# A Fourier mix and a maxout layer on one core: batch 0's first stage in two halves of output rows, and GpSimd's start-up work in another order

## The chip, the cores and the metric

The kernel runs on 1 core of one Trainium2 chip. The metric is the time of one execution on the device in microseconds; the time before is the median of 3 runs, 405.07 us (405.0 to 405.21). A profile is of one execution. Times inside it are counted from its first instruction.

Short names: PE is TensorE (matmuls; PEld its weight loads), DVE is VectorE, ACT is ScalarE, POOL is GpSimd, SP is SyncE, which here only asks for DMAs.

## The reference

```python
X = np.fft.fft(x, axis=1)          # x: 8 batches, 3072 positions, 256 channels, float32
X = np.fft.fft(X, axis=2)
t = X.real.astype(np.float32).reshape(24576, 256)
h = np.maximum(np.maximum(t @ w1, t @ w2), t @ w3)    # 256 -> 768
out = (h @ w_out).astype(np.float32)                   # 768 -> 256
```

## The kernel before, in words

**The work of one batch.** The Fourier transform over 3072 positions is split into 24 by 128. Stage one (`Mix.s`, seven pieces k = 0 to 6) multiplies x, as the stationary operand of 96 rows (4 channel groups of 24 positions) by 128 columns, with small constant matrices of at most 96 columns; the result is evicted into `z`. Stage two (`Mix.k`, pieces 0 to 5) multiplies `z` with the sine and cosine table `tabs` and gives `t`, the halves tE and tO. The transform over the channels is folded into the weights: `prep_first` multiplies the differences d2 = w2 - w1 and d3 = w3 - w1 (held in `d2_bf`, `d3_bf`; `differences`, line 231, makes them) with the matrix `md` and leaves `gE`, `gO` and `gD`, one of each for d2 and for d3. It does so for the halves jh = 0 and jh = 1 of the 768 columns, the second inside the unit loop. `prep_second` makes the folded output weights `gw` from `w1` and `w_out`.

**The unit loop.** For each of 8 batches there are 3 blocks of 512 tokens, and for each of them 6 units (jc). A unit (`unit_plus`) is four matmuls into two PSUM tiles, `pse2` and `pse3`; `unit_out` takes them out: ACT writes the Relu of `pse2` into `stmp` (line 605), then DVE takes the maximum of `stmp` and `pse3` (line 606). One unit later, two `gD` matmuls (`unit_minus`) turn the same PSUM tiles into the mirrored tokens, and `unit_out` runs again. `l2_block` multiplies with `w_out` and stores the rows, half of them through an indirect DMA that POOL issues with the row numbers in `rows_m`.

**What sets the order.** The schedule is manual on all five engines: each engine runs its instructions in the order in which the program emits them, and waits on semaphores. `plan` says behind which unit a side piece (stage one and two of the next batch, transposing copies, table pieces) is emitted. For batch 0, unit 2 emits `tab_sines(10, 13, (0,))` on ACT, which reads the table angles `w_late` that POOL's `tab_angles(10, 13)` has written; unit 4 emits the matmuls that read `wout_bf`.

**The start, which the diff touches.** Batch 0's x comes through POOL's DMA queue in three parts of positions bb (rows 0 to 40, 40 to 80, 80 to 112; four DMAs each, one per channel group), and the last 16 rows through SP and ACT. Each part is laid out twice by ACT and DVE, forward into `xn0` (`lay_rows`) and reversed into `xr0` (`turn_rows`). Behind x, POOL asks for w1; SP asks for the four pieces of w2 and w3 (`raw_w`: w2 and w3 of jh = 0, then of jh = 1) once the ninth of x's twelve DMAs (`last_part[0]`) has landed. 28 matmuls on dummy data (line 774) run until x is laid out. Then PE runs stage one, and behind its pieces stand d2 and d3 of jh = 0 on DVE, d2 and d3 of jh = 1 on POOL, the DMA for `w_out` and `tab_angles(10, 13)` on POOL. POOL's order before them is: a marker that waits for x's layout (line 460), four memsets, `store_rows` (the row numbers for the stores, lines 278 to 288), `tab_minus(7, 10)` (line 343).

**A pool that closes.** `pidx`, `rows_f` and `late`, which `store_rows` reads and writes, are tiles of the pool `gen`. That pool is closed before the unit loop, and the pools opened behind it (`h_pool` with `stmp`, `hp` and `hm` among them) take its place in SBUF:

```python
gen_pool_cm.__exit__(None, None, None)      # line 802
ps_s_cm.__exit__(None, None, None)
...
h_pool = ctx.enter_context(tc.tile_pool(name="hbuf", bufs=2))
```

Of the kernel before, what the change touches and what calls it, by code (L numbers as in the profile page):

```python
# [9 lines left out]
FP32 = mybir.dt.float32  # L10
# [3 lines left out]
ALU = mybir.AluOpType  # L14
# [19 lines left out]
def kernel(  # L34
# [221 lines left out]
    iota(pidx, [[0, 1]], cm=1)  # L256
    j128 = gen.tile([128, 128], FP32, tag="j128")
    iota(j128, [[1, 128]])
    for (r0, r1) in ((0, 40), (40, 80), (80, 112)):
        last_part = load_rows(nc.gpsimd, x0v[:, r0:r1, :], 0, r0, r1)  # L260

    def load_w(eng, wdst, wsrc, jh):
        return eng.dma_start(
            out=cols(wdst, jh),
            in_=wsrc.rearrange("(fc p) j -> p fc j", fc=2)[:, :, jh * 384:(jh + 1) * 384])

    for jh in range(2):
        load_w(nc.gpsimd, w1_bf, moe_w1, jh)
    for jh in range(2):
        for wsrc, wdst in zip((moe_w2, moe_w3), raw_w):  # L270
            ld = load_w(nc.sync, wdst, wsrc, jh)
            if jh == 0:
                tc.add_manual_dep(ld.ins, last_part[0].ins.name, AFTER, reason="x first")

    rows_f = gen.tile([128, 7 * B], FP32, tag="rows_f")
    late = gen.tile([128, 1], FP32, tag="late")
# [135 lines left out]
    def turn_rows(copy, r0, n, d0, d1):  # L412
        return reverse(copy, xr0, x0_first[:, r0 * 64:(r0 + n) * 64], r0, n, d0, d1)
# [32 lines left out]
    turn_rows(on_dve, 39, 40, 32, 65)  # L446
    lay_rows(on_act, bf_rows(40, 40), 40, 40, 12, 33)
    second_laid = lay_rows(on_dve, bf_rows(40, 40), 40, 40, 0, 12)
    for (copy, a, b, c, d) in ((on_act, 55, 64, 21, 33), (on_dve, 32, 55, 0, 21)):
        third_turned = turn_rows(copy, 79, 33, a, b)  # L450
        if copy is on_act:
            turn_rows(copy, 79, 32, 64, 65)
        laid = lay_rows(copy, bf_rows(80, 32), 80, 32, c, d)
    nc.vector.tensor_scalar(out=sgn, in0=pidx, scalar1=0.0, scalar2=None, op0=ALU.is_equal)
    nc.vector.tensor_scalar(out=sgn, in0=sgn, scalar1=2.0, scalar2=-1.0,
                            op0=ALU.mult, op1=ALU.add)
    nc.vector.tensor_scalar(out=dif, in0=sgn, scalar1=1.0, scalar2=None, op0=ALU.subtract)
    for ch in range(4):
        raw[1, ch] = load_chunk(1, ch)
    first_op = nc.gpsimd.memset(mark, 0.0)  # L460
    tc.add_manual_dep(first_op.ins, laid.ins.name, AFTER, reason="the two share a port")
    nc.gpsimd.memset(two_row, 0.0)
    nc.gpsimd.memset(two_row[0:1], 2.0)
    nc.gpsimd.memset(gw[:, 512:513], 0.0)
    nc.gpsimd.memset(gw[0:1, 512:513], 1.0)
    store_rows()
    tab_minus(7, 10, nc.gpsimd)

    def wide(t, cs):
        return t.rearrange("p (fc j) -> p fc j", fc=2)[:, :, cs]  # L470

    def prep_first(jh, bank):

        cs = slice(jh * 384, (jh + 1) * 384)
        for i, wv in enumerate((d2_bf, d3_bf)):
            for half in range(2):
                psg = bank()
                hs = slice(half * 128, (half + 1) * 128)
                for fc in range(2):
                    nc.tensor.matmul(  # L480
                        psg[:, 0:384], md[fc][:, hs],
                        wv[:, fc * DFF + jh * 384: fc * DFF + jh * 384 + 384],
                        start=(fc == 0), stop=(fc == 1))
                if half == 0:
                    nc.vector.tensor_copy(out=gE[i][:, cs], in_=psg[:, 0:384])
                else:
                    nc.scalar.copy(out=gO[i][:, cs], in_=psg[:, 0:384])
                    nc.vector.tensor_scalar(out=gD[i][:, cs], in0=psg[:, 0:384], scalar1=dif,
                                            scalar2=None, op0=ALU.mult)
                yield  # L490

    def prep_second():
# [30 lines left out]
    class Mix:  # L523
# [4 lines left out]
            self.tE = self.t[:, 0, :]  # L528
            self.tO = self.t[:, 1, :]

        def s(self, k, x0, pool=ps_f, evict=nc.scalar.copy):

            ps1 = pool.tile([128, 512], FP32, name="ps1", tag="ps")
            if k < len(DLS):
                parts = [(d, 96, m24f, m24r) for d in range(*DLS[k])]
            else:
                parts = [(0, 52, m0f, m0r), (32, 48, m24f, m24r), (1, 96, m24f, m24r)]
            c0 = 0
            for (d, n, mf, mr) in parts:
                if isinstance(x0, tuple):  # L540
                    pairs = ((x0[0](d), mf), (x0[1](d), mr))
                elif d:
                    pairs = ((x0[:, d, :], mf),)
                else:
                    pairs = ((x0[:, 0, :], mf), (x0[:, 33, :], mr))
                for i, (st, mv) in enumerate(pairs):
                    nc.tensor.matmul(ps1[:, c0:c0 + n], st, mv[:, 0:n], start=(i == 0),  # L547
                                     stop=(i == len(pairs) - 1))
                c0 += n
            if k < len(DLS):  # L550
                lo = 4 * DLS[k][0]
                evict(out=z[:, lo:lo + 20, 0:24],  # L552
                      in_=ps1[:, 0:480].rearrange("p (c r) -> p c r", r=24))
            else:
                evict(out=z_all[:, 0:52], in_=ps1[:, 0:52])
                evict(out=z[:, 2:8, 0:24],
                      in_=ps1[:, 52:196].rearrange("p (c r) -> p c r", r=24))

        def k(self, q, evict=nc.scalar.copy, pool=ps_f):

# [24 lines left out]
    def unit_plus(te, to, jc, n):  # L585
# [4 lines left out]
        for (pse, i) in ((pse2, 0), (pse3, 1)):  # L590
            nc.tensor.matmul(pse[:, 0:n], gE[i][:, js], te, start=True, stop=False)  # L591
            nc.tensor.matmul(pse[:, 0:n], gO[i][:, js], to, start=False, stop=True)  # L592
        return pse2, pse3
# [175 lines left out]
                l2_queue.pop(0)  # L769

    warm = ps_s.tile([128, 512], FP32, name="warm", tag="ps")
    for (n, after) in ((23, None), (3, second_laid), (2, third_turned)):
        for i in range(n):
            mm = nc.tensor.matmul(warm, tab[:, 0:128], tab[:, 0:512], start=True, stop=True)
            if after is not None and i == 0:
                tc.add_manual_dep(mm.ins, after.ins.name, AFTER, reason="warm until x is laid out")
    m = Mix(0)
    x0f = (lambda d: xn0[:, d, 0:128], rows_back(xr0))
    for k in range(7):
        m.s(k, x0f, pool=ps_s if k % 4 else ps_f,  # L780
            evict=nc.vector.tensor_copy if k in (1, 3) else nc.scalar.copy)
        if k == 1:
            halves = [t.rearrange("p (q two g) -> p two q g", two=2, g=4) for t in md]
            nc.vector.tensor_copy(out=halves[1][:, 0], in_=halves[0][:, 0])
            nc.vector.tensor_scalar(out=halves[1][:, 1], in0=halves[0][:, 1], scalar1=-1.0,
                                    scalar2=None, op0=ALU.mult)
            differences(nc.vector, 0, (0,))
        if k == 3:
            first_half = differences(nc.vector, 0, (1,))
            differences(nc.gpsimd, 1, after=first_half)  # L790
            nc.gpsimd.dma_start(out=wout_bf.rearrange("p (jc c) -> p jc c", jc=NJC),
                                in_=moe_w_out.rearrange("(jc p) c -> p jc c", jc=NJC))
# [100 lines left out]
    for b in range(B):  # L893
# [15 lines left out]
        for blk in range(3):  # L909
# [5 lines left out]
                for t, fl in zip((tE, tO), flipped):  # L915
                    nc.gpsimd.tensor_copy(fl, t[:, 3 * TOKB - 1: 2 * TOKB - 1: -1])
            for jc in range(NJC):
                pses = unit_plus(tE[:, cs], tO[:, cs], jc, TOKB)
# [52 lines left out]
```

## Time and profile before

| | |
|---|---|
| median of 3 runs | 405.07 us |
| the profiled execution | 404.64 us |
| its span, first to last instruction | 402.9 us |
| PE busy in the span | 386.0 us (96%) |
| DVE, ACT, POOL busy | 308.9, 265.5, 292.0 us |
| first dummy matmul | 10.01 us |
| first matmul of stage one | 18.67 us |
| first matmul of the unit loop | 24.18 us |

The profiled execution's time is 1.7 us over its span: what lies around the first and the last instruction. It is 0.43 us under the median. Rows of the timeline read: start, duration, engine, line, operation, output tile <- input tiles, shapes, count; in square brackets the engine's idle time before it and what ended it. A row with a count merges neighbours that are the same.

### The profile page before, as it was taken

The page shows a single profiled execution, that of the slowest core. Times are in us where ns is not written, and L with a number is a line of the kernel's source. Part 1 is how long each engine was busy: PE and PEld are TensorE (multiplying, and loading weights), DVE is VectorE, ACT ScalarE, POOL GpSimd, SP SyncE. Part 2 cuts the span into 40 slices and gives each one's busy share as a digit, 9 for nine tenths or more (in the row PEclk, how much of TensorE's full clock was granted, in tenths as well). Part 3 has the DMA queues.
Part 4 walks back from the last instruction along what each step waited for, and adds up shares of the span by engine and source line. Part 5 has one row for each costly group of instructions (what it writes and reads, how often), then busy time and mean ns, then how long its engine had stood idle before and what let it go on. Part 6 is the DMA issues. An engine that isn't in the chain of part 4 may idle for free.

```text
span 402.9 us, 8560 instructions
## 1 busy us (share of the span) xinstructions
PE 386.0 (96%) x2829; PEld 260.6 (65%) x2877; DVE 308.9 (77%) x556; ACT 265.5 (66%) x489; POOL 292.0 (72%) x394
## 2 busy tenths in 40 slices
PE   0999999999999999999999999999999999999996
PEld 0465667666676667666666666666677676666665
DVE  8898776788777877687776887787777877678884
ACT  6787767655866667756766677666766676655550
POOL 9599889879986998679877888768967524323521
PEclk9999999999999999999999999999999999999999
DMA  9989897789778838875478928886234411211214
GB/s 117 188 199 179 157 226 197 174 213 196 186 197 214 192 120 217 193 184 159 114 200 186 227 78 222 197 191 179 81 103 114 123 55 74 84 52 54 103 57 156
DMA packets 127597, 62.06 MB, mean 154 GB/s; under 512 B 111616, under 2 KB 116736, under 8 KB 126976
## 3 DMA queue, kind: packets, MB, share of 16 engines
q1 hardware_dynamic: 101976, 42.21, 42.3%
q0 software_dynamic: 24640, 18.98, 23.8%
q8 instruction: 22, 0.36, 0.4%
q10 hardware_dynamic: 936, 0.33, 0.3%
q14 instruction: 23, 0.19, 0.2%
HBM read 33.74 MB, written 29.88 MB: 158 GB/s over the span
## 4 chain that ended last, share of the span: by engine, by line
PE 85%; DVE 4%; DMA 3%; POOL 2%; ACT 2%; issue 2%; DVEq 0%; SPq 0%; POOLq 0%; ACTq 0%
PE po L616 29%; PE pse L591 16%; PE pse L599 14%; PE pse L592 12%; PE ps L571 3%; PE ps L573 3%; PE po L640 3%; PE pl L629 2%; PE ps L547 2%; POOL x L111 2%; DMA raw_w<-in_moe_w_dram 2%; DVE hm L606 2%; ACT stmp L605 2%; DMA x<-in_x_dram 2%; DVE other L643 1%
## 5 line engine op out<-in xcount | busy, mean ns | idle before, releaser
L605 ACT ACTIVATE stmp<-pse 128x512 bf16<-128x512 f32 x288 | 170.8, 600 | 52.6 <-PE pse L592 26.2
L606 DVE TENSOR_TENSOR hp<-pse,stmp 128x512 bf16<-128x512 f32 x144 | 99.5, 691 | 80.1 <-ACT stmp L605 51.8
L646 POOL TENSOR_TENSOR even<-even,other 128x256 f32<-128x256 f32 x92 | 70.1, 762 | 74.5 <-DVE other L643 74.2
L591 PE MATMUL pse<-t,gE 128*128 128x512 bf16 x288 | 109.1, 379 | 2.5
L606 DVE TENSOR_TENSOR hm<-pse,stmp 128x512 bf16<-128x512 f32 x144 | 99.2, 689 | 3.3 <-ACT stmp L605 3.1
L592 PE MATMUL pse<-t,gO 128*128 128x512 bf16 x249 | 94.3, 379 | 0.0
L616 PE MATMUL po<-wout_bf,hp 128*128 128x256 bf16 x576 | 85.9, 272 | 0.0
L616 PE MATMUL po<-wout_bf,hm 128*128 128x256 bf16 x570 | 85.3, 273 | 0.3
L599 PE MATMUL pse<-t,gD 128*128 128x512 bf16 x279 | 83.7, 379 | 0.1
L677 POOL DMA_INDIRECT out_dram<-ot,rows_m x53 | 53.8, 1015 | 20.2 <-DVE ot L670 10.7
L616 PEld LDWEIGHTS <-hp 128*128 128x128 bf16 x576 | 56.3, 98 | 17.3 <-issue 2.5
L616 PEld LDWEIGHTS <-hm 128*128 128x128 bf16 x576 | 56.4, 98 | 16.5
L670 DVE TENSOR_TENSOR ot<-po,even 128x512 f32<-128x512 f32 x92 | 62.8, 682 | 0.0
L173 POOL CAST xw<-xs 96x544 bf16<-96x544 f32 (+1 forms) x48 | 53.2, 1120 | 0.0
L178 POOL CAST xb<-xs 96x512 bf16<-96x512 f32 x48 | 52.4, 1100 | 0.0
L575 ACT CAST t<-ps 128x512 bf16<-128x512 f32 x48 | 27.9, 585 | 34.8 <-PE ps L573 34.7
L599 PEld LDWEIGHTS <-gD 128*128 128x128 bf16 x288 | 28.1, 98 | 32.2
L643 DVE SCALAR_TENSOR_TENSOR other<-twice,po 128x256 f32<-128x256 f32 x92 | 43.8, 476 | 0.1
L592 PEld LDWEIGHTS <-gO 128*128 128x128 bf16 x288 | 28.1, 98 | 20.4 <-issue 1.9
L591 PEld LDWEIGHTS <-gE 128*128 128x128 bf16 x288 | 28.2, 98 | 19.5 <-issue 0.7
L552 ACT CAST z_all<-ps 128x480 bf16<-128x480 f32 x46 | 24.8, 560 | 22.0 <-PE ps L547 21.9
L632 ACT COPY even<-pl 128x512 f32<-128x512 f32 x46 | 27.0, 587 | 9.7 <-PE pl L629 8.6
(178 smaller groups left out, 370.9 us busy)
## 6 DMA issues: line engine op xcount, KB each, us to landing
xs<-in_x_dram SPq DMA_DIRECT2D x84, 198.0 KB
out_dram<-ot SPq DMA_DIRECT2D x39, 256.0 KB
xs<-in_x_dram SPq DMA_DIRECT2D x28, 192.0 KB
held<-xb SPq DMA_DIRECT2D x48, 96.0 KB
xw<-held POOLq DMA_DIRECT2D x24, 192.0 KB
raw_w<-in_moe_w_dram SPq DMA_DIRECT2D x4, 384.0 KB
out_dram<-ot SPq DMA_DIRECT2D x12, 128.0 KB
x<-in_x_dram POOLq DMA_DIRECT2D x8, 120.0 KB
```

The lines of the kernel that those rows point to most:

```text
L173: nc.gpsimd.tensor_copy(v[:, d0:d1, ch * 32:ch * 32 + 32], xs[:, 0:32 * 64].rearrange("p (bb dl) -> p dl bb", dl=64)[:, d0:d1, :])
L178: nc.gpsimd.tensor_copy(mir[:, d0:d1, c0:c0 + 32], bass.AP(xs.tensor, xs.offset + 33 * 64 - 1 - d0, [xs.ap[0], [-1, d1 - d0], [-64, 32]]))
L591: nc.tensor.matmul(pse[:, 0:n], gE[i][:, js], te, start=True, stop=False)
L592: nc.tensor.matmul(pse[:, 0:n], gO[i][:, js], to, start=False, stop=True)
L599: nc.tensor.matmul(pse, gD[i][:, js], to, start=False, stop=True, skip_group_check=True)
L605: nc.scalar.activation(out=stmp[:, 0:n], in_=pses[0][:, 0:n], func=AX.Relu)
L606: nc.vector.tensor_tensor(out=dst, in0=src3, in1=stmp[:, 0:n], op=ALU.max)
L616: nc.tensor.matmul(po, hcols(jc), wout_bf[:, jc * 256:(jc + 1) * 256], start=False, stop=(jc == NJC - 1), skip_group_check=True)
L643: nc.vector.scalar_tensor_tensor(out=other, in0=twice, scalar=po[:, 256:257], in1=po[:, 0:256], op0=ALU.mult, op1=ALU.subtract)
L646: nc.gpsimd.tensor_tensor(out=line[:, 256:512], in0=line[:, 0:256], in1=other, op=ALU.add)
L670: nc.vector.tensor_tensor(out=parts, in0=po.rearrange("p (i c) -> p i c", i=2), in1=lin.rearrange("p (i c) -> p i c", i=2), op=ALU.add)
L677: stored(nc.gpsimd.indirect_dma_start(out.rearrange("(n two) c -> n (two c)", two=2) if pair else out, bass.IndirectOffsetOnAxis(ap=rows_m ...
```

## The change

Batch 0's stage one is made in two passes over its seven pieces, with seven PSUM banks open (`banks_s`). `s_half` with `sooner` makes 64 columns of x forward (rows 0 to 64) into PSUM partitions 0 to 63 and 64 columns reversed into partitions 64 to 127; these need x's rows up to 64 only. One dummy matmul waits for the third part's reversal. `s_half` with `later` adds the other 64 columns of each, crosswise, and after each piece `s_out` evicts it, odd pieces by DVE and even ones by ACT. Instead of 66 matmuls with 128 stationary columns there are 132 with 64.

x's parts are cut at row 84 instead of 80. SP asks for the weight pieces, w3's ahead of w2's, once the eighth x DMA (`parts_first[3]` of the second part) has landed.

d3 of jh = 0 moves from DVE to POOL, ahead of everything else there but the marker; d2 of jh = 0 stays on DVE, behind the evictions of stage one; on POOL follow d3 and d2 of jh = 1. The four memsets and `sgn` and `dif` go ahead of the marker on POOL. `store_rows` and `tab_minus(7, 10)` go behind the differences. `prep_first` takes d3 ahead of d2, and for jh = 0 makes both `gD` products at its end. Unit 0 takes `pse3` ahead of `pse2`. Stage two's piece 1 is evicted by DVE.

```diff
-    for (r0, r1) in ((0, 40), (40, 80), (80, 112)):
-        last_part = load_rows(nc.gpsimd, x0v[:, r0:r1, :], 0, r0, r1)
+    for (r0, r1) in ((0, 40), (40, 84), (84, 112)):
+        parts_first = load_rows(nc.gpsimd, x0v[:, r0:r1, :], 0, r0, r1)
+        if r0 == 40:
+            before_last = parts_first[3]
...
+    nc.gpsimd.tensor_scalar(out=sgn, in0=pidx, scalar1=0.0, scalar2=None, op0=ALU.is_equal)
+    nc.gpsimd.tensor_scalar(out=sgn, in0=sgn, scalar1=2.0, scalar2=-1.0,
+                            op0=ALU.mult, op1=ALU.add)
+    nc.gpsimd.tensor_scalar(out=dif, in0=sgn, scalar1=1.0, scalar2=None, op0=ALU.subtract)
+    nc.gpsimd.memset(two_row, 0.0)
+    nc.gpsimd.memset(two_row[0:1], 2.0)
+    nc.gpsimd.memset(gw[:, 512:513], 0.0)
+    nc.gpsimd.memset(gw[0:1, 512:513], 1.0)
     for jh in range(2):
-        for wsrc, wdst in zip((moe_w2, moe_w3), raw_w):
+        for wsrc, wdst in ((moe_w3, raw_w[1]), (moe_w2, raw_w[0])):
             ld = load_w(nc.sync, wdst, wsrc, jh)
             if jh == 0:
-                tc.add_manual_dep(ld.ins, last_part[0].ins.name, AFTER, reason="x first")
+                tc.add_manual_dep(ld.ins, before_last.ins.name, AFTER, reason="x first")
...
-            turn_rows(copy, 79, 32, 64, 65)
-        laid = lay_rows(copy, bf_rows(80, 32), 80, 32, c, d)
+            turn_rows(copy, 83, 28, 64, 65)
+        laid = lay_rows(copy, bf_rows(84, 28), 84, 28, c, d)
+
+    def sooner(d):
+        return xn0[:, d, 0:64], (xr0[:, 32 - d, 64:128] if d else xr0[:, 32, 65:129])
+
+    def later(d):
+        return xn0[:, d, 64:128], (xr0[:, 32 - d, 0:64] if d else xr0[:, 32, 1:65])
...
     tc.add_manual_dep(first_op.ins, laid.ins.name, AFTER, reason="the two share a port")
-    nc.gpsimd.memset(two_row, 0.0)
-    nc.gpsimd.memset(two_row[0:1], 2.0)
-    nc.gpsimd.memset(gw[:, 512:513], 0.0)
-    nc.gpsimd.memset(gw[0:1, 512:513], 1.0)
-    store_rows()
-    tab_minus(7, 10, nc.gpsimd)
...
-        for i, wv in enumerate((d2_bf, d3_bf)):
+        for i, wv in ((1, d3_bf), (0, d2_bf)):
...
-                    nc.vector.tensor_scalar(out=gD[i][:, cs], in0=psg[:, 0:384], scalar1=dif,
-                                            scalar2=None, op0=ALU.mult)
+                    scaled.append((gD[i][:, cs], psg[:, 0:384]))
+                if half and (jh or not i):
+                    for (dst, product) in scaled:
+                        nc.vector.tensor_scalar(out=dst, in0=product, scalar1=dif,
+                                                scalar2=None, op0=ALU.mult)
+                    scaled = []
...
+        def s_half(self, k, rows, ps1):
+
+            begin = rows is sooner
+            if k < len(DLS):
+                parts = [(d, 96, m24f, m24r) for d in range(*DLS[k])]
+            else:
+                parts = [(0, 52, m0f, m0r), (32, 48, m24f, m24r), (1, 96, m24f, m24r)]
+            c0 = 0
+            for i, (d, n, mf, mr) in enumerate(parts):
+                for j, (st, mv) in enumerate(zip(rows(d), (mf, mr))):
+                    p0 = 64 * j if begin else 64 - 64 * j
+                    nc.tensor.matmul(ps1[p0:p0 + 64, c0:c0 + n], st, mv[:, 0:n],
+                                     start=begin and i == 0,
+                                     stop=not begin and i == len(parts) - 1,
+                                     skip_group_check=True)
+                c0 += n
...
-    for (n, after) in ((23, None), (3, second_laid), (2, third_turned)):
...
+    warm_up(22)
     m = Mix(0)
...
+    for k in range(7):
+        m.s_half(k, sooner, banks_s[k])
+    warm_up(1, third_turned)
+    for k in range(7):
+        m.s_half(k, later, banks_s[k])
+        m.s_out(k, banks_s[k], nc.vector.tensor_copy if k % 2 else nc.scalar.copy)
         if k == 1:
...
-            differences(nc.vector, 0, (0,))
-        if k == 3:
-            first_half = differences(nc.vector, 0, (1,))
-            differences(nc.gpsimd, 1, after=first_half)
-            nc.gpsimd.dma_start(out=wout_bf.rearrange("p (jc c) -> p jc c", jc=NJC),
-                                in_=moe_w_out.rearrange("(jc p) c -> p jc c", jc=NJC))
-            tab_angles(10, 13, nc.gpsimd)
+            differences(nc.gpsimd, 0, (1,))
+    first_half = differences(nc.vector, 0, (0,))
+    differences(nc.gpsimd, 1, (1, 0), after=first_half)
+    store_rows()
+    tab_minus(7, 10, nc.gpsimd)
+    nc.gpsimd.dma_start(out=wout_bf.rearrange("p (jc c) -> p jc c", jc=NJC),
+                        in_=moe_w_out.rearrange("(jc p) c -> p jc c", jc=NJC))
+    tab_angles(10, 13, nc.gpsimd)
...
-    m.k(1, pool=ps_s)
+    m.k(1, pool=ps_s, evict=nc.vector.tensor_copy)
```

More of the change, by code (lines that the diff above doesn't have):

```diff
@@ L445 @@
     nc.scalar.activation(out=md[0], in_=vm, func=AX.Sin, scale=float(-2.0 * math.pi / 256.0))
-    turn_rows(on_dve, 39, 40, 32, 65)
-    lay_rows(on_act, bf_rows(40, 40), 40, 40, 12, 33)
-    second_laid = lay_rows(on_dve, bf_rows(40, 40), 40, 40, 0, 12)
+    turn_rows(on_dve, 39, 44, 32, 65)
+    lay_rows(on_act, bf_rows(40, 44), 40, 44, 12, 33)
+    lay_rows(on_dve, bf_rows(40, 44), 40, 44, 0, 12)
+    halves = [t.rearrange("p (q two g) -> p two q g", two=2, g=4) for t in md]
+    nc.vector.tensor_copy(out=halves[1][:, 0], in_=halves[0][:, 0])
+    nc.vector.tensor_scalar(out=halves[1][:, 1], in0=halves[0][:, 1], scalar1=-1.0,
+                            scalar2=None, op0=ALU.mult)
     for (copy, a, b, c, d) in ((on_act, 55, 64, 21, 33), (on_dve, 32, 55, 0, 21)):
-        third_turned = turn_rows(copy, 79, 33, a, b)
+        third_turned = turn_rows(copy, 83, 29, a, b)
         if copy is on_act:
-            turn_rows(copy, 79, 32, 64, 65)
-        laid = lay_rows(copy, bf_rows(80, 32), 80, 32, c, d)
[L454 to L457, printed above, removed]
+            turn_rows(copy, 83, 28, 64, 65)
[4 more added lines that the diff above has]
+        return xn0[:, d, 64:128], (xr0[:, 32 - d, 0:64] if d else xr0[:, 32, 1:65])
     for ch in range(4):
@@ L487, in prep_first @@
                     nc.scalar.copy(out=gO[i][:, cs], in_=psg[:, 0:384])
-                    nc.vector.tensor_scalar(out=gD[i][:, cs], in0=psg[:, 0:384], scalar1=dif,
-                                            scalar2=None, op0=ALU.mult)
+                    scaled.append((gD[i][:, cs], psg[:, 0:384]))
+                if half and (jh or not i):
+                    for (dst, product) in scaled:
+                        nc.vector.tensor_scalar(out=dst, in0=product, scalar1=dif,
+                                                scalar2=None, op0=ALU.mult)
+                    scaled = []
                 yield
@@ L529, in __init__, with s @@
             self.tO = self.t[:, 1, :]
-        def s(self, k, x0, pool=ps_f, evict=nc.scalar.copy):
+        def s(self, k, x0, pool=ps_f):
             ps1 = pool.tile([128, 512], FP32, name="ps1", tag="ps")
@@ L549, in s, with s_out @@
                 c0 += n
+            self.s_out(k, ps1)
+        def s_out(self, k, ps1, evict=nc.scalar.copy):
             if k < len(DLS):
@@ L583, in end, with unit_plus @@
             nc.scalar.copy(out=t_mid[:, :, self.b], in_=ps3[:, 0:2])
-    def unit_plus(te, to, jc, n):
+    def unit_plus(te, to, jc, n, swap=False):
         js = slice(jc * 128, (jc + 1) * 128)
@@ L589, in unit_plus @@
         pse3 = ps_l1.tile([128, TOKB], FP32, name="pse3", tag="pse3")
-        for (pse, i) in ((pse2, 0), (pse3, 1)):
+        for (pse, i) in ((pse2, 0), (pse3, 1)) if swap is False else ((pse3, 1), (pse2, 0)):
             nc.tensor.matmul(pse[:, 0:n], gE[i][:, js], te, start=True, stop=False)
@@ L771, with warm_up @@
     warm = ps_s.tile([128, 512], FP32, name="warm", tag="ps")
-    for (n, after) in ((23, None), (3, second_laid), (2, third_turned)):
+    def warm_up(n, after=None):
         for i in range(n):
@@ L776 @@
                 tc.add_manual_dep(mm.ins, after.ins.name, AFTER, reason="warm until x is laid out")
+    warm_up(22)
     m = Mix(0)
-    x0f = (lambda d: xn0[:, d, 0:128], rows_back(xr0))
+    banks_s = [(ps_s if k % 4 else ps_f).tile([128, 512], FP32, name="ps1", tag="ps")
+               for k in range(7)]
     for k in range(7):
-        m.s(k, x0f, pool=ps_s if k % 4 else ps_f,
-            evict=nc.vector.tensor_copy if k in (1, 3) else nc.scalar.copy)
-        if k == 1:
[L783 to L786, printed above, removed]
-            differences(nc.vector, 0, (0,))
-        if k == 3:
-            first_half = differences(nc.vector, 0, (1,))
-            differences(nc.gpsimd, 1, after=first_half)
-            nc.gpsimd.dma_start(out=wout_bf.rearrange("p (jc c) -> p jc c", jc=NJC),
-                                in_=moe_w_out.rearrange("(jc p) c -> p jc c", jc=NJC))
-            tab_angles(10, 13, nc.gpsimd)
+        m.s_half(k, sooner, banks_s[k])
[3 more added lines that the diff above has]
+        m.s_out(k, banks_s[k], nc.vector.tensor_copy if k % 2 else nc.scalar.copy)
+        if k == 1:
+            differences(nc.gpsimd, 0, (1,))
[6 more added lines that the diff above has]
+    tab_angles(10, 13, nc.gpsimd)
     slots = [ps_s, ps_s, ps_f, ps_f]
@@ L917 @@
             for jc in range(NJC):
-                pses = unit_plus(tE[:, cs], tO[:, cs], jc, TOKB)
+                pses = unit_plus(tE[:, cs], tO[:, cs], jc, TOKB, (b, blk, jc) == (0, 0, 0))
                 unit_out(pses, hp[:, jc, :], TOKB)
```

## The prediction

> **What bounds the kernel now.** First the table by stretches, then the chain of waits, then the timelines of POOL and ACT at the start. The stretches (from:to, length, then each engine's busy time with its instructions in the order PE, PEld, DVE, ACT, POOL, then PE's clock, the DMA share and GB/s), two of the start and one of the steady part:
>
> ```profile
> 18.67:21.51 2.84, 2.84 (x67) 2.75 (x67) 2.05 (x7) 1.64 (x4) 2.42 (x12) 1.00 1.02 360
> 21.51:24.18 2.67, 2.57 (x19) 1.62 (x17) 2.67 (x5) 2.38 (x8) 2.13 (x3) 1.00 0.93 208
> 100.00:200.00 100.00, 99.08 (x736) 67.61 (x746) 76.11 (x131) 67.78 (x127) 85.52 (x116) 1.00 0.72 178
> ```
>
> In the steady part PE is busy for 99.08 of 100 us, so whatever the first units lose or gain is carried to the end. The change touches nothing behind them: it is worth what it does to unit 0 to 4 of batch 0. The chain of waits there (start, duration, what):
>
> ```profile
> 8.76 6.22 DMA x<-in_x_dram
> 15.01 0.42 SPq L263
> ...
> 15.98 7.10 DMA raw_w<-in_moe_w_dram
> ...
> 23.25 1.65 POOL d_bf L233
> 24.90 0.04 issue
> 24.94 0.61 ACT stmp L605
> ...
> 27.43 0.57 issue
> ...
> 29.12 0.22 PE pse L592
> ```
>
> It does not pass through stage one. It goes from the ninth x DMA (landed at 8.76 + 6.22 = 14.98) to SP's request for the weights, to the landing of their third piece at 15.98 + 7.10 = 23.08, and through POOL to unit 0's first Relu at 24.94. The start is bound by the weights' transfer.
>
> **The change, part by part.**
>
> *The weights' request* now waits for the eighth x DMA. x's rows of all DMAs share the DMA engines, so I count packets (24 per row and DMA). Before, the ninth ended 8 x 960 + 768 = 8448 packets, and the last of 10752 released ACT and DVE at 17.0:
>
> ```profile
> 17.01 0.86 ACT L144 COPY back<-x 96x297 bf16<-96x297 bf16 x2 [0.73 <-DMA x<-in_x_dram]
> 17.78 0.74 DVE L419 COPY nat<-x 96x672 bf16<-96x672 bf16 x1
> 18.67 0.20 PE L547 MATMUL ps<-m24f,nat 96*128 96x96 bf16 x1
> ```
>
> That is (17.01 - 14.98) / 2304 = 0.88 ns a packet. With part two cut at row 84 the eighth ends 4 x 960 + 4 x 1056 = 8064 packets, 384 fewer: 0.34 us sooner. The DMA engines are full in that stretch (share 1.02), so the pieces land between 0 and 0.34 us sooner; I take 0.34, the third at 22.74. x itself is as many packets; weights that cut in ahead of its last rows may cost 0 to 0.3 us, hidden as shown next. Batch 1's x, next in SP's queue, is asked for as much sooner and is not waited for here.
>
> *Stage one in halves*: 132 matmuls with 64 stationary columns, 66 in each half. No row shows such a one. The 66 of before took 2.84 us, 0.042 each. Lower and upper bound:
>
> ```profile
> 21.22 0.19 PE L547 MATMUL ps<-m0f,nat 96*128 96x52 bf16 x1
> 21.32 0.20 PE L547 MATMUL ps<-m24f,nat 96*128 96x96 bf16 x1
> 21.32 0.10 PEld L547 LDWEIGHTS <-back 96*128 96x128 bf16 x1
> 10.01 7.73 PE L774 MATMUL warm<-tab 128*128 128x512 bf16 x26 [10.01 <-DVE tab L343]
> ```
>
> From 21.22 to 21.32 run four matmuls of 52 and 48 columns with their loads: 0.025 each, the lower end, if the two column halves work side by side. A load takes 0.10; with only two in flight, one for each half, 0.049 is the upper end. I take 0.036, between the lower end and the nearest row. `sooner` starts behind 22 dummy matmuls (26 end at 17.74; four at 0.22 less, and a tail of 0.16: 16.7) and ends at 19.1; one dummy; `later` runs from 19.3 to 21.7. Part three, 28 rows instead of 32 to lay out, is ready near 18.4 and is not waited for. Stage one ends 0.2 us later than the 21.51 of before (20.2 at the lower price, 23.4 at the upper).
>
> [...]
>
> *d3 on POOL, and d3's product first.* The rows of before:
>
> ```profile
> 20.49 0.96 DVE L233 TENSOR_TENSOR d_bf<-raw_w,w_bf 128x768 bf16<-128x768 f32 x1
> 22.36 0.33 PE L571 MATMUL ps<-tab,z_all 128*128 128x256 bf16 x1
> 23.27 0.61 DVE L488 TENSOR_SCALAR gD<-psg,dif 128x384 bf16<-128x384 f32 x1
> ```
>
> The first piece had landed by 20.49, now 20.15; POOL needs 1.64 (half of the 3.24 below) where DVE took 0.96, so d3 is there at 21.8. Its four matmuls (0.65) stand ahead of stage two, which starts at 22.5 instead of 22.36. Nothing is gained by then, and with both `gD` (0.61 each) moved ahead of DVE's first maximum unit 0 loses another 0.5 to 1. That is covered by what follows; if the cover is gone, it is the price.
>
> *POOL's order.* This decides:
>
> ```profile
> 18.59 0.09 POOL L460 MEMSET mark<- 1x1 f32 x1 [4.17 <-DVE sgn L454]
> 19.22 0.45 POOL L245 IOTA rows_f<- 128x40 f32 x3
> 20.73 0.81 POOL L288 CAST rows_m<-rows_f 128x56 int32<-128x56 f32 x1
> 21.52 1.19 POOL L343 TENSOR_SCALAR tab<-tab 128x384 bf16<-128x384 bf16 x1
> 23.25 3.24 POOL L233 TENSOR_TENSOR d_bf<-raw_w,w_bf 128x768 bf16<-128x768 f32 x2 [0.54 <-DMA raw_w<-in_moe_w_dram]
> 26.44 0.91 POOL L791 DMA_DIRECT2D wout_bf<-in_moe_w_out_dram  x1
> 27.37 0.85 POOL L319 TENSOR_TENSOR w_late<-pi_all,step 128x384 f32<-128x384 f32 x1
> 29.57 1.00 POOL L329 TENSOR_TENSOR w_late<-w_high,w_late 128x384 f32<-128x384 f32 x1
> ```
>
> The memsets, `sgn` and `dif` go into the 4.17 us in which POOL waited: free. But `store_rows` (19.22 to 21.52, 2.30 us) and `tab_minus` (1.19) lay beside the weights' transfer, with 0.54 us left idle. Now they come behind the subtractions, with nothing beside them. Two readers are near. The first Relu writes `stmp`, in a pool that takes the place of `gen`, whose last user on POOL is `store_rows`; ACT's list of waits shows that it waits for POOL:
>
> ```profile
> ACT stmp L605 <- POOL d_bf L233: 0.3, 1, 0.3
> ```
>
> The row names the subtraction because that was POOL's latest signal; the Relu reads nothing of it, and by the code the pool's last user is meant. The second reader is the sine of `w_late` on ACT, 0.15 us behind `tab_angles` (29.57 + 1.00), without slack:
>
> ```profile
> 30.24 0.59 ACT L575 CAST t<-ps 128x512 bf16<-128x512 f32 x1
> 30.72 0.53 ACT L335 ACTIVATE tab<-w_late 128x384 bf16<-128x384 f32 x1
> 34.48 1.47 PE L509 MATMUL psw<-wout_bf,g1t 128*128 128x256 bf16 x12
> ```
>
> Behind both stands ACT's whole queue, the Relus of all later units, and PE runs out of free banks two units on.
>
> *The sum.* POOL's subtractions for jh = 1 wait for their piece (22.74 + 0.17, as 23.08 to 23.25: 22.9) and for d2 on DVE (piece 5 of stage one 21.55, eviction 0.65, subtraction 0.96: 23.2); the later is 23.2. Then 3.24, so 26.4; `store_rows` 2.30, so 28.7; the Relu at 28.8 instead of 24.94: 3.86 later. PE and POOL get ahead in the meantime, but DVE's work behind the Relu is as much as before; of the 0.57 us of idle time in the chain I let 0.16 be won back. Net +3.7. `w_late` is ready at 28.7 + 1.19 + 4.13 (26.44 to 30.57) = 34.0 and is wanted at 30.72 + 3.7 = 34.4; `w_out` is asked for at 29.9 instead of 26.44, took 8.0 us at most (read at 34.48), and is wanted at 38.2: neither adds. The profiled execution, 404.64, becomes 408.3; its median is 0.43 higher, 405.07, so I predict 408.8.
>
> **The rivals.**
>
> *Faster: the weights come in time.* If the pieces come so early that POOL's moved work ends before the Relu is due, stage one's gain shows: at the lower price `z` is done about 1.2 us sooner, 403.9. It decides where `store_rows` ends by 23.9, the subtractions by 21.6, the third piece landed by 18.2. The row of 23.08 and a request 0.34 us sooner speak against it.
>
> *The Relu waits for something else on POOL.* Then the sine decides: 26.4 + 2.30 + 1.19 + 4.13 + 0.15 = 34.15 against 30.72, +3.4, or 3.2 if d2 isn't late: 408.4.
>
> *The halves are bound by weight loads.* At 0.049 `later` ends at 23.4, d2 at 24.85, `store_rows` at 30.4: +5.3, 410.4.
>
> *The delay is made good.* ACT and DVE have idle time behind unit 4; should half of the delay be won back there, 406.9. PE's 99 of 100 us speak against it.
>
> **How the numbers follow.** Main case 0.58, 408.8, with prices from 0.025 to 0.042 a matmul 408.5 to 409.4; Relu free of `store_rows` 0.14; load-bound halves 0.12; made good in part 0.06; faster 0.07; within 0.2% 0.03. About 0.2% (0.8 us) is what a measurement can tell from no change. The range 407.0 to 411.0 holds the first three cases, with the upper price, and leaves out 0.16. Faster 0.07, same 0.03, slower 0.90.
>
> **What would show it.** Right: POOL's row of L288 near 28 instead of 20.73; the first Relu near 28.8 with ACT idle for 3 us or more before it, ended by POOL; PE idle between units 1 and 2; the steady part as before. Wrong: the third weight piece landed before 21, the first Relu before 25, or the matmuls of `later` at 0.049 or more.

## The result, and the profile after

The changed kernel takes 408.02 us (median of 6 executions, 407.65 to 408.38); the kernel before, measured beside it, 404.96 us. The ratio is 1.0078 (95% interval 1.0065 to 1.0091): 3.06 us slower, by 0.8%. The prediction was 408.8 (407.0 to 411.0). In the experiments below, one execution of e4 (679.89 us, at a mean clock of 0.573) and two of the first six of e3 (over 1.5% above the fastest) were slow ones and are left out of the ratios. The profiled execution of after took 408.38, 3.74 more than the one of before; its span is 406.6 us against 402.9.

First the chain of waits of after (start, duration, what), to be held against the chain of before:

```profile
14.53 0.42 SPq L265
...
16.01 9.47 DMA raw_w<-in_moe_w_dram
25.55 1.64 POOL d_bf L233
27.18 0.42 POOL rows_f L245 x3
...
28.63 0.24 POOL rows_m L298
28.89 0.61 ACT stmp L642
```

The chain still goes from the weights' transfer through POOL's subtraction to the first Relu. But now it hangs on the last piece (25.48) instead of the third, and between the subtraction and the Relu stands `store_rows` (lines 245 to 298). The Relu starts at 28.89 instead of 24.94. The lists of waits of after (engine, line, tile, what it waited for: us in total, times, longest) name both ends of it:

```profile
ACT stmp L642 <- POOL rows_m L298: 3.6, 1, 3.6
PE psg L492 <- POOL d_bf L233: 1.9, 1, 1.9
PE pse L628 <- DVE gD L503: 1.1, 1, 1.1
```

ACT stood idle for 3.6 us in front of its first Relu, and the row now names the writer of `rows_m` itself, where before it named the subtraction. The other two rows are PE's own waits, for d3 and for the late `gD`; they matter below. POOL's timeline of after:

```profile
14.87 1.24 POOL L274 TENSOR_SCALAR dif<-sgn 128x1 f32<-128x1 f32 x1
16.70 0.78 POOL L277 MEMSET gw<- 128x1 bf16 x1
18.14 0.09 POOL L477 MEMSET mark<- 1x1 f32 x1
20.76 1.64 POOL L233 TENSOR_TENSOR d_bf<-raw_w,w_bf 128x768 bf16<-128x768 f32 x1 [2.53 <-DMA raw_w<-in_moe_w_dram]
23.46 1.64 POOL L233 TENSOR_TENSOR d_bf<-raw_w,w_bf 128x768 bf16<-128x768 f32 x1 [1.06 <-DMA raw_w<-in_moe_w_dram]
25.55 1.64 POOL L233 TENSOR_TENSOR d_bf<-raw_w,w_bf 128x768 bf16<-128x768 f32 x1 [0.44 <-DMA raw_w<-in_moe_w_dram]
```

Each of the three subtractions waits for its piece of the weights, 2.53, 1.06 and 0.44 us: POOL is bound by landings, and has 2.5 us free between its marker and the first of them, where `store_rows` used to be.

The two halves of stage one and the steady part, by stretches (from:to, length, busy time and instructions of PE, PEld, DVE, ACT, POOL, then PE's clock, DMA share, GB/s):

```profile
17.16:18.64 1.48, 1.48 (x67) 1.45 (x66) 0.93 (x2) 0.70 (x1) 0.95 (x3) 1.00 0.97 242
18.98:20.30 1.32, 1.32 (x63) 1.32 (x64) 0.66 (x2) 0.87 (x2) 0.00 (x0) 1.00 1.03 357
100.00:200.00 100.00, 99.85 (x747) 67.74 (x746) 76.49 (x131) 67.46 (x125) 85.46 (x115) 1.00 0.73 177
```

The first half takes 1.48 us, 0.022 a matmul; in the steady part PE is as full as before (99.85 of 100 us for 99.08).

### The profile page after: what moved, and what is told of

Read it like the earlier page. It is cut to its first block, busy times and chain, and to the rows that moved or that the text cites. A ratio compares the mean times of both kernels' runs of the same rounds, so it can differ in the third digit from the quotient of the medians.

```text
span 406.6 us, 8729 instructions
## 1 busy us (share of the span) xinstructions
PE 388.7 (96%) x2938; PEld 260.5 (64%) x2938; DVE 309.0 (76%) x554; ACT 264.2 (65%) x487; POOL 296.2 (73%) x398
## 4 chain that ended last, share of the span: by engine, by line
PE 91%; DMA 4%; POOL 2%; DVE 1%; ACT 0%; issue 0%; SPq 0%; POOLq 0%; ACTq 0%
PE po L653 31%; PE pse L628 15%; PE pse L636 15%; PE pse L629 15%; PE ps L563 3%; PE po L677 3%; PE ps L610 3%; PE ps L608 3%; PE pl L666 2%; DMA raw_w<-in_moe_w_dram 2%; DMA x<-in_x_dram 2%; POOL x L111 2%; POOL d_bf L233 0%; DVE hm L643 0%; SPq L265 0%
## 5 line engine op out<-in xcount | busy, mean ns | idle before, releaser
L629 PE MATMUL pse<-t,gO 128*128 128x512 bf16 x288 | 109.0, 379 | 0.0
L636 PE MATMUL pse<-t,gD 128*128 128x512 bf16 x288 | 85.8, 379 | 1.4 <-ACT stmp L642 1.1
```

Source lines behind the costliest of these rows:

```text
L636: nc.tensor.matmul(pse, gD[i][:, js], to, start=False, stop=True, skip_group_check=True)
```

## The experiments

All are measured against the kernel before on the same chip: e1 to e4 on one chip, after again, e6, e5 and the second run of e3 on another, e7 to e9 on a third, e10 on a fourth. The times are medians.

| run | what it is | us | ratio to before (95%) |
|---|---|---|---|
| e2 | before, with the two calls late | 408.85 | 1.0082 (1.0055 to 1.0110) |
| e1 | after, both calls back | 408.77 | 1.0076 (1.0049 to 1.0102) |
| e3 | after, three tiles with the constants | 426.99, again 429.74 | 1.0488 (1.0438 to 1.0538), 1.0583 (1.0513 to 1.0653) |
| e4 | before, with the halves | 406.25 | 1.0027 (1.0010 to 1.0044) |
| after again | the changed kernel | 408.00 | 1.0075 (1.0051 to 1.0099) |
| e6 | after, the two calls in POOL's gaps | 408.42 | 1.0075 (1.0045 to 1.0104) |
| e5 | e4, stage two ahead of the products | 405.77 | 1.0019 (1.0007 to 1.0032) |
| e7 | e6 with PE kept busy | 406.43 | 1.0037 (1.0025 to 1.0049) |
| e9 | after with PE kept busy | 407.68 | 1.0069 (1.0054 to 1.0085) |
| e8 | e3 with a pad | 408.18 | 1.0077 (1.0054 to 1.0100) |
| e10 | e7, stage two ahead, ACT evicts | 406.12 | 1.0026 (1.0014 to 1.0038) |

**The late calls alone (e2).** The kernel before, with only this moved:

```diff
-    store_rows()
-    tab_minus(7, 10, nc.gpsimd)
...
             differences(nc.gpsimd, 1, after=first_half)
+            store_rows()
+            tab_minus(7, 10, nc.gpsimd)
```

> The kernel before with only store_rows and tab_minus moved behind POOL's two subtractions. Theory A: subtractions end at 26.5, store_rows at 28.8, first Relu 28.85 instead of 24.94, waiting for POOL; +3.7 us, 408.7. Theory B: nothing in unit 0 changes, 405.0.

408.85 is the expected 408.7, but not by the order alone. Four of the six executions had a mean PE clock of 0.996 and took 408.61 to 409.79; the two at a clock of 1.0 took 407.38 and 407.83. So the move by itself costs 2.2 to 2.7 us over the 405.15 of before on that chip, and the lower clock, whose stretch is shown at the end, goes with the rest. That the sum came out at 408.85 is luck in part. ACT's timeline of e2 shows the same wait as after's:

```profile
28.01 0.60 ACT L603 ACTIVATE stmp<-pse 128x512 bf16<-128x512 f32 x1 [3.32 <-POOL rows_m L288]
```

So the order of POOL's queue is enough to make most of the loss. It doesn't follow that it makes as much of it in the changed kernel, where other work is late too.

**The calls back in after (e1).**

```diff
     first_op = nc.gpsimd.memset(mark, 0.0)
...
+    store_rows()
+    tab_minus(7, 10, nc.gpsimd)
...
-    store_rows()
-    tab_minus(7, 10, nc.gpsimd)
```

> The changed kernel with store_rows and tab_minus put back right behind the marker on POOL; all else as changed. Theory A (these two, behind the weight-bound subtractions, hold the first Relu): store_rows runs from 18.2 to 20.5 and tab_minus to 21.7, d3 is 0.9 us later than in the changed kernel, the first Relu comes near 27.0 instead of 28.89 and waits for PE, not for POOL; 406.3, some 1.7 us under the changed kernel and 1.3 over the one before. Theory B (d3 on POOL ahead of stage two and the products at DVE's end cost it, not POOL's order): d3 is later still, so 408.5 or more.

408.77: the gain that I expected is not in the time. The wait is gone, though. ACT's timeline of e1:

```profile
30.07 0.60 ACT L644 ACTIVATE stmp<-pse 128x512 bf16<-128x512 f32 x1 [1.52 <-PE pse L631]
```

The Relu waits for PE now, not for POOL, and is still late. One of the six executions took 406.76 us, the others 408.28 to 409.55; the one had a mean PE clock of 0.999, the others 0.995 or 0.996. That was the first sign of a second cause. In PE's timeline of e1 the third weight's products stand behind a wait of 3.28 us, since POOL reached d3 only after both calls, at 22.41:

```profile
24.66 0.81 PE L494 MATMUL psg<-d_bf,md_all 128*128 128x384 bf16 x4 [3.28 <-POOL d_bf L233]
```

and in the table by stretches of e1 PE runs at half clock soon after:

```profile
26.50:28.04 1.54, 1.54 (x6) 0.44 (x3) 1.24 (x3) 0.03 (x1) 1.54 (x2) 0.50 0.83 153
```

**The calls in POOL's gaps (e6).** `store_rows` fits between the marker and d3, `tab_minus` behind d3, so that neither delays a subtraction:

```diff
     first_op = nc.gpsimd.memset(mark, 0.0)
...
+    store_rows()
...
             differences(nc.gpsimd, 0, (1,))
+            tab_minus(7, 10, nc.gpsimd)
...
-    store_rows()
-    tab_minus(7, 10, nc.gpsimd)
```

> The changed kernel with only POOL's order changed: store_rows right behind the marker, where POOL waits 2.5 us for the first weight piece, and tab_minus behind d3 of jh = 0, where it waits 1.1 us for the third; d3 is not delayed. Theory A (their place holds the first Relu): the Relu waits for PE alone and starts near 27.0 instead of 28.89; 406.1, 1.9 us under the changed kernel. What is left over the kernel before, 1.1 us, is then the price of d3 on POOL and of the products' order. Theory B (POOL's order does not matter, the rest does): 408.0.

408.42: no gain again, and all four executions had a clock of 0.992 to 0.996. In the profiled one x's second part (rows 40 to 84) came late: ACT and DVE waited for it until 16.26, and stage one began at 18.27, after PE had been idle for 2.00 us. By stretches of e6:

```profile
18.27:19.84 1.57, 1.57 (x66) 1.52 (x67) 1.46 (x4) 1.33 (x3) 0.00 (x0) 1.00 1.12 355
20.75:22.98 2.23, 2.22 (x58) 2.14 (x55) 1.46 (x3) 1.67 (x3) 1.99 (x5) 0.50 0.99 348
```

The first half ran at full clock, the second at 0.50, 0.038 us a matmul where the first took 0.024.

**PE kept busy (e7), and its control (e9).** e7 is e6, e9 is after, each with eight dummy matmuls more:

```diff
-    warm_up(22)
+    warm_up(26)
...
+    warm_up(4)
     first_half = differences(nc.vector, 0, (0,))
```

> The kernel of e6 (store_rows behind the marker, tab_minus behind the third weight's first difference) with TensorE kept busy by matmuls that nothing reads: four more ahead of x's last rows (26 for 22) and four between stage one and the third weight's products. Theory A: the readers in gen's place are worth the 1.7 us expected of e6, and e6 lost them because TensorE stood idle for 2 us and then ran at half clock in every one of its executions (mean clock 0.992 to 0.996). Then the clock is 1.0 here and the time 406.3 us (405.9 to 406.9). Rival B: with x's last rows landing as they do, the place of the two readers is not worth anything once the halves are there; the time stays at 408.0 to 408.4, whatever the clock. Rival C: the matmuls come in the way of the halves; over 408.5.

> The changed kernel with the same eight matmuls and nothing else: the control for e7. Its clock is 1.0 in most executions already and its first Relu waits for GpSimd's store_rows, which these matmuls don't touch. Theory A: 408.0 us (407.5 to 408.4), as the changed kernel. Rival B (a cold TensorE is a part of the changed kernel's loss too): 407 or less.

e7 took 406.43, all of its nine executions at a clock of 0.999 or 1.0; e9, on the same chip, 407.68. By stretches of e7 the second half of stage one stays at full clock:

```profile
19.80:21.38 1.58, 1.57 (x66) 1.52 (x68) 0.92 (x2) 1.13 (x3) 0.07 (x1) 1.00 1.06 389
```

Both times lie in theory A's ranges. Of the 3.03 us that e9 loses against before (407.68 - 404.65), the place of the two calls is worth 1.25 (407.68 - 406.43), less than the 1.7 expected; 1.78 are left when it is undone. The profiles show the same step. The weights landed later in e7's profiled execution, the slowest of its nine, so the first Relu has to be counted from the start of d3 on POOL. POOL's d3 and ACT's first Relu, of e7, then of e9:

```profile
21.68 1.65 POOL L233 TENSOR_TENSOR d_bf<-raw_w,w_bf 128x768 bf16<-128x768 f32 x1 [1.81 <-DMA raw_w<-in_moe_w_dram]
28.05 0.60 ACT L643 ACTIVATE stmp<-pse 128x512 bf16<-128x512 f32 x1 [1.82 <-PE pse L630]
```

```profile
20.50 1.64 POOL L233 TENSOR_TENSOR d_bf<-raw_w,w_bf 128x768 bf16<-128x768 f32 x1 [2.60 <-DMA raw_w<-in_moe_w_dram]
28.18 0.60 ACT L642 ACTIVATE stmp<-pse 128x512 bf16<-128x512 f32 x1 [3.13 <-POOL rows_m L298]
```

That is 6.37 us in e7, where the Relu waits for PE, and 7.68 in e9, where it waits for `rows_m`: 1.31 more. Since e7 differs from e6 by the eight matmuls alone, the clock is what had hidden this gain in e6. In e1 d3 was late as well, and the two were not separated. In the changed kernel run again a lower clock shows less: its executions at 1.0 took 407.09 and 408.00, those at 0.995 or 0.996 took 407.16, 408.07 and 409.06.

**Who waits for POOL: the Relu through `gen`'s place (e3, e8).** If the three tiles of `store_rows` lie with the constants, no tile of `h_pool` takes their place, and only the readers by value (the sine of `w_late`, and what reads `w_out`) are left:

```diff
-    pidx = gen.tile([128, 1], FP32, tag="pidx")
+    pidx = consts.tile([128, 1], FP32, tag="pidx")
...
-    rows_f = gen.tile([128, 7 * B], FP32, tag="rows_f")
-    late = gen.tile([128, 1], FP32, tag="late")
+    rows_f = consts.tile([128, 7 * B], FP32, tag="rows_f")
+    late = consts.tile([128, 1], FP32, tag="late")
```

> The changed kernel with pidx, rows_f and late held outside the pool gen, so that nothing of store_rows is waited for when gen's place is used again; POOL's order unchanged. The first Relu should start near 26.7. If the sine of w_late has no slack (the second reader), ACT then waits for POOL there until 34.2 and only 0.2 to 0.4 us are gained, 407.7; if the Relu's wait alone was the loss, 2.2 us are gained, 405.8.

> The changed kernel with pidx, rows_f and late outside the pool gen, once more, since x came 6 us later in the first look. First Relu near 27.0 without a wait for POOL. If the sine of w_late has no slack: ACT waits there for POOL until 34.2, 1 to 2 us, and the time is 407.4 to 407.8; if the Relu's wait alone was the loss, 406.1.

Both runs are some 20 us slow, by something that neither theory had. The constants stand in front of x's buffers in SBUF, so the three tiles there shift these by 288 bytes. e8 adds a pad of 224 bytes, so that the shift becomes 512, and nothing else:

```diff
+    consts.tile([128, 56], FP32, name="pad", tag="pad")
     pidx = consts.tile([128, 1], FP32, tag="pidx")
```

> The kernel of e3 (pidx, rows_f and late held with the constants, out of gen's place) with 224 bytes of padding, so that the 288 bytes that e3 added in front of x's buffers become 512. Theory A (the place of x's buffers made e3 slow, since its transfers into SBUF no longer began at multiples of 512 bytes): x's last rows land at 14 to 16 us again instead of 20, and the time is 406 to 408.5 us. Rival B (holding the three tiles with the constants is itself what costs, or the buffers' place as such): 420 us or more, as e3. If A holds, the first Relu no longer waits for GpSimd's rows_m, and the time against the changed kernel's 408.0 is one more measure of the two readers: 406.3 if they set the first Relu alone.

408.18. So the shift by 288 bytes was it, not that the three tiles lie with the constants. The table of DMA queues (packets, MB, share of 16 engines' span) of e3's second run, then that of e8:

```profile
q1 hardware_dynamic: 101976, 42.21, 51.1%
q0 software_dynamic: 24640, 18.98, 31.3%
```

```profile
q1 hardware_dynamic: 101976, 42.21, 42.0%
q0 software_dynamic: 24640, 18.98, 23.1%
```

A share is of the span, 427.7 us in e3's second run and 406.5 in e8. So the same packets and the same bytes took 1.28 times as long on SP's and ACT's queue (51.1% of 427.7 against 42.0% of 406.5) and 1.43 times on POOL's. At the start, by stretches, 98 GB/s against 131, first e3's second run, then e8:

```profile
4.00:14.00 10.00, 4.32 (x11) 1.56 (x12) 5.68 (x32) 5.60 (x14) 6.90 (x9) 1.00 3.74 98
```

```profile
4.00:14.00 10.00, 4.33 (x11) 1.57 (x12) 9.23 (x39) 8.86 (x16) 10.00 (x12) 1.00 2.22 131
```

That x's buffers are the ones that count, and which shifts other than 512 would have been harmless, and so whether it is multiples of 512 bytes that count, was not separated.

For the readers e8 is the run to read. ACT's timeline of e8, then a row of its list of waits between 26 and 46 us:

```profile
26.49 0.60 ACT L643 ACTIVATE stmp<-pse 128x512 bf16<-128x512 f32 x1 [1.73 <-PE pse L630]
...
33.44 0.52 ACT L346 ACTIVATE tab<-w_late 128x384 bf16<-128x384 f32 x1 [1.31 <-POOL w_late L340]
```

```profile
PEld L526 <- DMA wout_bf<-in_moe_w_out_dram: 1.0, 1, 1.0
```

The first Relu waits for PE only and starts at 26.49, 1.7 us ahead of e9's 28.18, whose last weights landed at the same time (24.75). So its wait for `rows_m` did come through `gen`'s place. Then the sine waits 1.31 us for `w_late`, and the time is what it was. But the sine is not alone in this: POOL also asked for `w_out` behind the late calls, at 29.25, it landed 8.7 us later, and the matmuls that read it began at 38.03, after 0.75 us in which PE stood idle. In e9 the same matmuls began at 37.47 without a wait; these 0.56 us are nearly the 0.61 by which e8's profiled execution (408.25) is longer than e9's (407.64). So there are three doors to the same late queue, the Relu, the sine and `w_out`. With the first one shut the other two together cost as much; what the sine alone costs was not measured.

**What the rest of the loss is (e4, e5, e10).** The kernel before with the halves alone, d2 and d3 of jh = 0 on DVE behind the evictions (e4), then with stage two ahead of the first two products (e5), then e7 with the same order and both of stage two's evictions on ACT (e10). The edit of e10:

```diff
-    next(first)
-    next(first)
     m.k(0, pool=ps_s)
-    m.k(1, pool=ps_s, evict=nc.vector.tensor_copy)
+    m.k(1, pool=ps_s)
+    next(first)
+    next(first)
```

> The kernel before with only stage one in two halves (its seven banks, evictions by turns on ACT and DVE, the differences behind them on DVE). If stage one bounds the start: z is done 1.1 us sooner and the time falls by about 1 us, 404.0. If the weights do (my reading): stage one ends near 20.4 but d2 and d3 stand behind the evictions on DVE until 22.4 and 23.4, stage two starts no sooner, and the time is within 0.5 us of before, 405.0 to 405.5.

> The kernel before with stage one in halves, and stage two's first two pieces ahead of d2's products in PE's queue (they no longer wait for d2, and d2 stands behind the evictions). Stage two runs from 21.4 to 22.3 instead of 23.8, beside d2 on DVE; the first Relu comes near 25.0 where the halves alone had 26.1. 405.0 if that wait is what the halves alone lost (1.1 us); 406.2 if not.

> The kernel of e7 with stage two of batch 0 (both calls of m.k) ahead of the third weight's products and both of its evictions on ScalarE. In e7 the first unit's matmul waits 1.1 us for the gD that VectorE makes behind one of these evictions (0.69 us), while ScalarE and TensorE stand idle until the third weight's difference is there. Theory A (behind the third weight's landing it is VectorE's queue that sets the first unit): the first unit starts some 0.55 us sooner and the time falls to 405.8 us (405.4 to 406.1), still over the kernel before. Rival B (what is left of the loss lies elsewhere, in the weights' transfer or in GpSimd's difference of 1.64 us where VectorE took 0.95): 406.4, as e7. Neither gives a time under the kernel before's 404.7 to 405.0.

e4's 406.25 is 1.0027 times before, over the 405.0 to 405.5 that I expected: the halves gain nothing and cost 1.1 us (406.25 - 405.15). The trace names a reason, that both differences stand behind DVE's evictions; PE waited 2.00 us for d2 before its first product at 22.95. DVE's and ACT's timelines of e4:

```profile
21.95 1.82 DVE L233 TENSOR_TENSOR d_bf<-raw_w,w_bf 128x768 bf16<-128x768 f32 x2
```

```profile
26.14 0.60 ACT L632 ACTIVATE stmp<-pse 128x512 bf16<-128x512 f32 x1 [0.32 <-PE pse L619]
```

Before, they ran at 20.49 and 21.93 between the evictions; here the second starts a microsecond later (21.95 + 0.91 = 22.86), and the first Relu 1.2 us later. In five of e4's eleven other executions the clock was 0.995 or 0.996, and these took 407.06 on average against 405.59 for the six at 1.0, 1.5 us more. So at full clock the halves cost some 0.4 us (405.59 - 405.15), and the lower clock, which goes with half of the executions, goes with the rest. e5 (405.77) and e10 (406.12, 405.12 to 407.41) lie between their two expectations and settle nothing; the intervals of e10 and e7 overlap. In e5's profile the first Relu came at 25.33, near the 25.0 expected and 0.81 sooner than in e4's, but the execution took as long (405.87 against 405.81).

That 1.78 us remain with the calls back is shown; how they divide between the halves, d3 on POOL and the late `gD` is open in the times. A profile points at `gD`. The list of waits of e8 has, in front of the first matmul of unit 0:

```profile
PE pse L629 <- DVE gD L504: 1.1, 1, 1.1
```

This matmul began at 25.37, before at 24.18. Of the 1.19 us between them the first product's later start makes 0.40 (21.91 for 21.51). Most of the rest is the wait of 1.1 us for `gD`; before, the longest wait for `gD` there, of PE's loads, was 0.2. No version here beats the kernel before.

## Why the prediction was right

**The main step, and its size.** "POOL's order. This decides": the first Relu was put at 28.8 with ACT idle for 3 us or more, ended by POOL; it is at 28.89 after 3.59 us, ended by `rows_m`. The mechanism is shown by e2, by e7 against e9, and by e8, where the wait is gone. That the size fits so well is luck: two errors in the sum made up for each other. I let POOL's last two subtractions run back to back from 23.2, held by d2 on DVE, and end at 26.4; in the profiled execution they waited for landings and ended at 27.19. (In the changed kernel run again and in e9 the first of the two did wait for d2, 0.89 us.) And I carried `store_rows` over at its 2.30 us of before; it takes 1.68 here (27.18 to 28.86). Nearly all of the difference is its last instruction (L288, now L298), which took 0.81 us before, beside a subtraction on DVE, and 0.23 here.

That the chain from the last landing through the Relu sets the end shows in three profiled executions with the late calls: after, and below the chain of the changed kernel run again and that of e9, one fence each.

```profile
15.83 8.33 DMA raw_w<-in_moe_w_dram
...
27.58 0.61 ACT stmp L642
```

```profile
15.50 9.26 DMA raw_w<-in_moe_w_dram
...
28.18 0.61 ACT stmp L642
```

The last piece landed at 24.16, 24.76 and 25.48, and the executions took 407.09, 407.64 and 408.38: 382.9 us more each time. This is also why the predicted 408.8 is 0.8 over the median. The +3.7 came out as +3.74 between the two profiled executions, but I added it to the median of before; after's profiled execution was the slowest of its six, and of the three here it had the latest weights.

**Where a step failed.** *The weights' request*: taken at 0.34 us, it was made 0.48 us sooner (14.53 for 15.01) and won nothing. The third piece, which I put at 22.74, was waited for until 23.46. The lower bound of 0 was the right end. My reason, that the DMA engines are full, is not shown: I took a share of 1.02 for full, but the share goes over 1 (2.22 at 131 GB/s in e8). What the chains show is that an earlier request was no earlier landing: asked for at 14.02, 14.35 and 14.53 in e9, the changed kernel run again and after, the last piece landed at 24.76, 24.16 and 25.48.

*The halves*: 0.036 a matmul was taken, 0.021 to 0.022 measured, under my lower end of 0.025. The timeline of PE's loads in after:

```profile
17.16 0.11 PEld L590 LDWEIGHTS <-nat 96*64 96x64 bf16 x1 [0.42 <-DVE md_all L461]
17.16 0.11 PEld L590 LDWEIGHTS <-back 96*64 96x64 bf16 x1
17.19 0.11 PEld L590 LDWEIGHTS <-nat 96*64 96x64 bf16 x1
17.19 0.11 PEld L590 LDWEIGHTS <-back 96*64 96x64 bf16 x1
```

The forward and the reversed load of a pair start together, and the matmuls likewise, so a pair costs what one matmul with 128 columns did (twice 0.021 to 0.022 us, for 0.042). Stage one ended at 20.56, a microsecond sooner than before (21.36 + 0.20 = 21.56) instead of 0.2 later. It was worth nothing, as said: PE then waited 1.9 us for d3. The upper bound's "only two in flight" was wrong too: a load takes 0.11 us, and pairs start every 0.04. The rival of load-bound halves (410.4) needed 0.049 a matmul and falls: 66 loads took 1.45 us, 22 ns each.

*d3 on POOL* was put at 21.8 and came at 22.40; stage two, put at 22.5, starts behind products that begin at 22.45. *The memsets, `sgn` and `dif`* were free, as said: they end at 18.1 and d3's weights come at 20.7. *Unit 0 "loses another 0.5 to 1", covered*: covered it was, but the price is larger. With the cover gone the Relu is at 26.49 (e8), 1.55 later than before, and 1.78 us remain in the time (e7). I had named the two `gD` and left out that the PSUM tiles of unit 0 take the place of d3's products, which a late `gD` still reads: the wait of 1.1 us in the list above.

**The rivals.** "The Relu waits for something else on POOL, then the sine decides, 408.4" is not what happened, but e8 makes that case. Its 408.18 is near the price, but not for the sine alone: PE's wait for `w_out` is in it. In after, that `w_late` and `w_out` don't add held: ACT's sine runs at 34.43 without a wait, I had 34.0 against 34.4, and the matmuls that read `w_out` run at 38.19 without a wait, I had 38.2. *Made good in part* (406.9) and *faster* (403.9) fall: of the 3.95 us by which the Relu is late in the profiled execution, 3.74 are found in its time.

## What to carry to other kernels

A piece of work that was hidden in an engine's wait for data can cost its full length once it is put behind that data, and it may have readers by place (a tile that takes over its buffer) beside the readers by value. When two chains are late by nearly as much, undoing one shows only the difference: here the first Relu was 3.95 us late, but putting the calls back was worth only 1.25 us, since the chain through PE was late as well (1.55 us at the first Relu of e8, 1.78 us in e7's time). The same queue can have several readers, and taking one away shows the next. An experiment that opens a gap on PE should be read with the granted clock beside it, and one that adds bytes in front of other buffers should be checked for what it moves.

## What the runs showed of the hardware that was not expected

**Half clock after some 2 us without matmuls, in some executions.** In e6 PE was idle for 2.00 us before 18.27 and ran at a granted clock of 0.50 from 20.18 on, 1.9 us after the gap; in e2 it was idle for 1.87 us, and by stretches of e2:

```profile
31.40:33.40 2.00, 2.00 (x7) 0.83 (x6) 1.10 (x3) 1.21 (x3) 1.92 (x3) 0.50 1.23 172
```

In after 1.90 us idle, and in e4's profiled execution 2.00, were without such a stretch: the clock was 1.00 from 20.30 to 28.89 in after and from 22.95 to 28.00 in e4. So gaps of 1.87 and 2.00 us came before half clock in two executions, and gaps of 1.90 and 2.00 us did not in two others; what decides between them was not shown.

**Buffers shifted by 288 bytes.** Shifting buffers by 288 bytes cost some 20 us (426.99 and 429.74 us against 408.18 with a shift of 512), and the same packets took 1.28 and 1.43 times as long.

**x's rows do not land at the same time in every execution.** With the same program up to there, the eighth x DMA landed at 14.52 in after (7.99 + 6.53) and at 14.33 in the changed kernel run again (7.99 + 6.34). DVE's copy of x's second part into `nat` began at 15.99 in after, at 15.82 in the changed kernel run again and at 17.62 in e6, and stage one at 17.16, 16.49 and 18.27. Why is open.
